# A second level of Strassen's form in the output product of a fused attention and SwiGLU kernel

## The chip, the core and the metric

The kernel runs on one core of one Trainium2 chip. A core has engines that run side by side: TensorE (PE in the profile, with its weight loads as PEld), VectorE (DVE), ScalarE (ACT), GpSimd (POOL), and SyncE (SP), whose queue issues nearly all DMA transfers here. Each engine takes its instructions in the order of the program and waits on semaphores for the others. The metric is the device time of one execution in microseconds (us); lower is better.

## The reference, cut to what matters

```python
# q, k, v: (8, 12, 448, 64) float32; g_q, g_k: (64,)
def rmsnorm(x, g):
    return x / np.sqrt(np.mean(x * x, axis=-1, keepdims=True) + 1e-06) * g
q_n, k_n = rmsnorm(q, g_q), rmsnorm(k, g_k)
scores = (1.0 / np.sqrt(64)) * np.matmul(q_n, k_n.transpose(0, 1, 3, 2))
attn = softmax(scores)
x = np.matmul(attn, v).transpose(0, 2, 1, 3).reshape(3584, 768)
# w_gate, w_val: (768, 1536); w_out: (1536, 768)
xn = x / np.sqrt(np.mean(x * x, axis=-1, keepdims=True) + 1e-06) * rms_g
g = xn @ w_gate
val = xn @ w_val
out = (g * (1.0 / (1.0 + np.exp(-g))) * val) @ w_out
```

All of it is float32. The weights arrive as float64 and are made float32 on the chip.

## The kernel before

The work is one attention block over 8 sequences (b = 0 to 7) of 448 tokens with 12 heads, taken as 48 pairs of heads (g), and one feed-forward block over the same tokens. The order of TensorE's work is written by hand: `pe(fn)` (L382) runs one step and counts it, `after(n, fn)` (L379) places a piece of work of another engine n steps later, and `fill` (L1155) puts feed-forward steps between the attention steps of a pair, as many as their cost asks for. While sequence b is in attention, the output product of sequence b-2 and then the gate and value products of sequence b-1 are worked off. In the last 200 us there is no attention left: the output product of sequence 6, the gate and value products of sequence 7 and its output product follow one another.

Gate and value products (`quad`, L907) use Strassen's form with one level: seven products p1 to p7 instead of eight, each of 12 matmuls 128 x 128 by 224 columns. One step is one product. The seven right-hand blocks per hidden chunk, with the sums T1 to T4 made once in sequence 1 (`derive`, L845), lie in DRAM in `kept` and are streamed for each sequence.

The output product (`out_strassen`, L1041) does the same with pairs of 128-token tiles: seven products, each of six matmuls by 384 columns, for two pairs in most sequences. `out_pairs` (L805) names the tiles; sequences 0 and 4 finish one pair only and carry the rest on, so sequences 2, 3, 5, 6 and 7 have four tiles each, and so has sequence 1. The left sums S1 to S4 are made on VectorE while the gate products run (`sums`, L975 to L986, for each of the six hidden chunks). Results leave PSUM through VectorE or ScalarE (L1059, L1066, L1064, L1073) and go to DRAM by L1028.

The hidden values h lie in 14 tiles that are taken from a list and given back (`free_h`, L705). Weights pass through 25 blocks of 128 x 384 (`free_w`, L706), two more once the conversion has ended. `uses` (L814) is the fixed list of all blocks that will be wanted; `ask` (L824) sends the next loads as long as more than four blocks stay free, and `used` (L890) gives a block back one step after its last matmul. PSUM has three banks for the feed-forward products (`ps_f`, L369). GpSimd adds the exponentials for the softmax sums (L555, L562), makes the powers of the norms (L506) and scales q (L511).

Of the kernel before, what the change touches and what calls it, by code (L numbers as in the profile page):

```python
# [8 lines left out]
F32 = mybir.dt.float32  # L9
# [16 lines left out]
BW = 384  # L26
# [309 lines left out]
def safe_scores(  # L336
# [25 lines left out]
    NW, NH = 25, 14  # L362
    const, small = pool("c_const", 1), pool("c_small", 4)
    qk_pool, v_pool, qn_pool, qkT_pool = pool("c_qk", 4), pool("c_v", 3), pool("c_qn", 1), pool("c_qkT", 2)
    e_pool, tmp, y_pool, rest_pool = pool("c_e", 11), pool("c_tmp", 1), pool("c_y", 2), pool("c_rest", 2)
    x_pool, s_pool, slots = pool("c_x", 4), pool("c_xs", 3), pool("c_slots", 1)
    raw_pool, cv_pool = pool("c_raw", 7), pool("c_cv", 4)
# [330 lines left out]

    def block_of(n, fc):

        return f"B{fc // NFP + 1}{n + 1}", fc % NFP
# [3 lines left out]
    free_h = [slots.tile([128, 512], F32, name=f"h{i}") for i in range(NH)]  # L705
    free_w = [slots.tile([128, BW], F32, name=f"w{i}") for i in range(NW)]  # L706

    def block():

        if free_w:  # L710
            return free_w.pop(0), free_w
        return free_h.pop(0), free_h

    def room(n):
        return len(free_w) + max(len(free_h) - 4, 0) >= n
# [48 lines left out]
    room_so, carried = [], []  # L764
    TURNS = len(pieces) + 7

    def home(key):
        if key[0] == "w":
            return kept[key[2], NAMES.index(key[3]), key[4]]
        return kept_o[NAMES.index(key[2]), key[3]]  # L770
# [4 lines left out]
    def convert():  # L775

        n = turn_of["n"]
        if n >= TURNS or not room(1):
            return False
        turn_of["n"] += 1  # L780
        if 0 <= n - 5 < len(pieces):
            key = pieces[n - 5][0]
            st[key] = block()
            lo, top = st.pop(("cv", n - 5))
            nc.gpsimd.tensor_tensor(data(key).bitcast(I32), top, lo, ALU.add)
        if 0 <= n - 4 < len(pieces):
            st["cv", n - 4] = join(*st.pop(("cv", n - 4)))
        if 0 <= n - 3 < len(pieces):
            st["cv", n - 3] = split(st.pop(("raw", n - 3)), n - 3)
        if n < len(pieces):  # L790
            st["raw", n] = load_raw(pieces[n][1])
        if 0 <= n - 7 < len(pieces):
            keep(pieces[n - 7][0])
        if turn_of["n"] == TURNS:

            free_w.extend(cv_pool.tile([128, BW], F32, name="top") for _ in range(2))
            whole = [raw_pool.tile([128, 2 * BW], F32, name="raw") for _ in range(7)]
            room_so.extend(whole[:6])
            homes = [whole[6][:, 0:BW], whole[6][:, BW:]] + [cv_pool.tile([128, BW], F32, name="top") for _ in range(2)]
            carried.extend(t[:, i * 128:(i + 1) * 128] for t in homes for i in range(3))  # L800
        return True
# [12 lines left out]
    uses = []  # L814
    for b in range(1, B):
        for fp in range(NFP):
            uses += [("w", b, fp, name, w) for name in (("B12", "B11", "B22", "B21") if b == 1 else ORDER) for w in range(2)]
            if b == 1:
                uses += [("wd", b, name, fp) for name in BLOCKS]
        uses += [("wo", b, name, c) for name in ORDER_O for c in range(NFP)]  # L820
# [3 lines left out]
    def ask():  # L824

        if turn_of["n"] < TURNS:
            return
        while asked["n"] < len(uses):
            key = uses[asked["n"]]
            keep_free = 4  # L830
            if key[1] == 1 and key[0] in ("w", "wd"):
                fp = key[2] if key[0] == "w" else key[3]
                keep_free = max(7 + 8 * fp - asked["derived"], 1)
            elif asked["derived"] < len(derived):
                return
            if key[0] == "wo" and key[2][0] == "T" and asked.get("sums_o", 0) < 4 * NFP:
                return
            if len(free_w) <= keep_free:
                return
            asked["n"] += 1  # L840
            asked[key] = now["t"]
            st[key] = block()
            nc.sync.dma_start(out=data(key), in_=home(key))
# [45 lines left out]

    def used(key):  # L890
        give_back(key)
        after(1, ask)
# [14 lines left out]
    def quad(b, fp):  # L907
# [21 lines left out]
        def rows(fc):  # L929
            return st["h", b, fc][:, shift:shift + S]  # L930

        def p1():
            bank["a"] = product(b, fp, "A11", "B11")
# [7 lines left out]
        def p2():  # L941
            product(b, fp, "A12", "B21", onto=bank["a"])
            for fc in (fp, fp + NFP):
                st["h", b, fc] = free_h.pop(0)
                if ("h", b - 1, fc) in st:

                    before = st.pop(("h", b - 1, fc))
                    if b % 2:
                        nc.gpsimd.tensor_copy(st["h", b, fc][:, 0:64], before[:, S - 64:S])
                    if carries(b - 1):  # L950
                        at = out_pairs(b - 1)[-1][1] + 1
                        nc.gpsimd.tensor_copy(carried[fc], before[:, at * 128:(at + 1) * 128])
                    free_h.append(before)
# [21 lines left out]
        def sums(pair):  # L975

            st["left_sums"] = now["t"]
            if pair < len(out_pairs(b)):
                if fp == 0:
                    st["so", b, pair] = {name: room_so[3 * pair + i].rearrange("p (c n) -> p c n", c=NFP)  # L980
                                         for i, name in enumerate(("S1", "S2", "S4"))}
                of = lambda name: left_o(b, pair, name, fp)
                nc.vector.tensor_tensor(of("S1"), of("A21"), of("A22"), ALU.add)
                nc.vector.tensor_tensor(of("S2"), of("S1"), of("A11"), ALU.subtract)
                nc.vector.tensor_tensor(of("S3"), of("A11"), of("A21"), ALU.subtract)
                nc.vector.tensor_tensor(of("S4"), of("A12"), of("S2"), ALU.subtract)  # L986

        def p3_last():
            p3()
            after(3, lambda: sums(0))  # L990
            after(5, lambda: sums(1))
# [5 lines left out]
    def project_out(b, n, i, part, last):  # L997
# [5 lines left out]
        for fc in range(part * each, (part + 1) * each):  # L1003
            nc.tensor.matmul(ps, lhsT=st["h", b, fc][:, i * 128:(i + 1) * 128], rhs=data(("wo", b, *block_of(n, fc))),  # L1004
# [25 lines left out]

    def left_o(b, pair, name, c):

        if name in ("S1", "S2", "S4"):
            return st["so", b, pair][name][:, c, :]
        row, col = (2, 1) if name == "S3" else (int(name[1]), int(name[2]))
        i, fc = out_pairs(b)[pair][row - 1], c + (col - 1) * NFP
        return carried[fc] if i < 0 else st["h", b, fc][:, i * 128:(i + 1) * 128]
# [3 lines left out]
    def out_strassen(b):  # L1041
# [45 lines left out]
        def step(name, which, half, last):  # L1087
# [5 lines left out]
            for c in range(3 * half, 3 * half + 3):  # L1093
# [5 lines left out]
                if last and b % 4 == 3 and name in ("T3", "T4"):  # L1099
                    free_h.append(st.pop(("h", b, c + (name == "T4") * NFP)))  # L1100
# [9 lines left out]

    def plain(fc):
# [3 lines left out]
        h = lambda: st["h", 0, fc][:, 0:S]  # L1115

        def step(w, half):
# [10 lines left out]
            if w == 0:  # L1128
                st["h", 0, fc] = free_h.pop(0)
# [14 lines left out]
    def out_items(b):  # L1144
        if b >= FIRST_O:
# [9 lines left out]
    def fill(n=None):  # L1155
# [8 lines left out]
        for _ in range(min(n, len(todo))):  # L1164
# [13 lines left out]
            if now["t"] - st["block"] > 4 and now["t"] != st.get("left_sums"):  # L1178
                left = 3 - sum(derive() for _ in range(3))
                for _ in range(left):  # L1180
                    derive_o()

# [219 lines left out]
```

## Time and profile before

| what | value |
|---|---|
| runs | 1598.54, 1598.49 and 1596.86 us, median 1598.49 |
| span of the profiled execution, first to last instruction | 1595.3 us, so that some 3.2 us of the median lie around it |
| granted TensorE clock | 0.999 |
| VectorE, ScalarE, GpSimd busy | 55%, 29%, 41% of the span |
| DMA | 273.28 MB, mean 171 GB/s |
| weight blocks loaded for gate and value, 192 KB each | 511 and 41 from `kept` |
| weight blocks loaded for the output product, 192 KB each | 296 and 22 from `kept_o` |
| median time from issue to landing of such a load | 2.6 to 2.9 us |
| median time of a store of such a block | 3.8 us to `kept`, 3.5 us to `kept_o` |

How to read the profile: the first figure of a group is its busy time in us, the second the mean duration of one instruction in ns. A float32 matmul of the program is two TensorE instructions with a weight load each. Durations of TensorE instructions overlap, so the time from one to the next is taken from runs of many. In a timeline a row gives the start, the length of the merged run, the engine, the line and what ended the idle time ahead of it.

### The profile page before, as it was taken

The page shows a single profiled execution, that of the slowest core. Times are in us where ns is not written, and L with a number is a line of the kernel's source. Part 1 is how long each engine was busy: PE and PEld are TensorE (multiplying, and loading weights), DVE is VectorE, ACT ScalarE, POOL GpSimd, SP SyncE. Part 2 cuts the span into 40 slices and gives each one's busy share as a digit, 9 for nine tenths or more (in the row PEclk, how much of TensorE's full clock was granted, in tenths as well). Part 3 has the DMA queues.
Part 4 walks back from the last instruction along what each step waited for, and adds up shares of the span by engine and source line. Part 5 has one row for each costly group of instructions (what it writes and reads, how often), then busy time and mean ns, then how long its engine had stood idle before and what let it go on. Part 6 is the DMA issues. An engine that isn't in the chain of part 4 may idle for free.

```text
span 1595.3 us, 21559 instructions
## 1 busy us (share of the span) xinstructions
PE 1571.9 (99%) x7286; PEld 1113.4 (70%) x7286; DVE 872.6 (55%) x1556; ACT 470.3 (29%) x940; POOL 660.1 (41%) x712
## 2 busy tenths in 40 slices
PE   8999999999999999999999999999999999999998
PEld 4344445687756887578865788667885688759974
DVE  6889898578822556236562354635563355613531
ACT  6746563232222222222232222323322222101010
POOL 6867877465334443344333443344542342000000
PEclk9999999999999999999999999999999999999999
DMA  7648474957746554465544655584554544456651
GB/s 207 209 148 260 162 252 125 287 188 242 250 142 204 154 156 121 140 205 156 154 119 143 204 154 148 149 267 131 161 145 124 176 141 139 119 178 212 174 151 55
DMA packets 261996, 273.28 MB, mean 171 GB/s; under 512 B 78836, under 2 KB 258804, under 8 KB 261876
## 3 DMA queue, kind: packets, MB, share of 16 engines
q1 hardware_dynamic: 260948, 271.61, 56.6%
q8 instruction: 60, 0.98, 0.3%
q14 instruction: 60, 0.49, 0.1%
q10 hardware_dynamic: 800, 0.20, 0.1%
q0 software_dynamic: 128, 0.00, 0.0%
HBM read 232.40 MB, written 39.32 MB: 170 GB/s over the span
## 4 chain that ended last, share of the span: by engine, by line
PE 78%; DVE 7%; DMA 1%; issue 1%; POOL 0%; SPq 0%; ACT 0%; DVEq 0%; POOLq 0%
PE ff L902 39%; PE ff L1094 22%; PE sc L545 6%; PE av L597 5%; PE sc L575 2%; PE den L610 2%; PE tr L527 1%; DVE top L747 1%; DVE top L748 1%; DVE top L746 1%; PE ff L1004 1%; DVE rd L618 1%; DVE h L925 0%; DVE h L924 0%; DMA w<-kept_o 0%
## 5 line engine op out<-in xcount | busy, mean ns | idle before, releaser
L902 PE MATMUL ff<-x,w 128*128 128x224 f32 x1878 | 381.5, 354 | 0.1
L902 PEld LDWEIGHTS ff<-x,w 128*128 128x128 f32 x1878 | 351.3, 190 | 15.3 <-issue 11.7
L555 POOL TENSOR_TENSOR es<-e 128x448 f32<-128x448 f32 x82 | 91.7, 1141 | 492.0 <-ACT e L549 492.0
L902 PE MATMUL ff<-xs,w 128*128 128x224 f32 x1374 | 281.7, 353 | 4.4 <-DVE w L858 2.9
L902 PEld LDWEIGHTS ff<-xs,w 128*128 128x128 f32 x1374 | 258.0, 190 | 8.7 <-issue 6.0
L562 POOL TENSOR_TENSOR es<-es,e 64x448 f32<-64x448 f32 (+1 forms) x164 | 191.9, 1181 | 6.3
L618 DVE RECIPROCAL rd<-rd 128x448 f32<-128x448 f32 x41 | 121.0, 2952 | 113.7 <-ACT rd L617 113.7
L549 ACT ACTIVATE e<-sc,rs 128x448 f32<-128x448 f32 x288 | 161.6, 635 | 50.2 <-PE sc L545 47.8
L1094 PE MATMUL ff<-w,h 128*128 128x384 f32 x498 | 167.8, 487 | 0.6 <-ACT p L1073 0.6
L1094 PE MATMUL ff<-w,raw 128*128 128x384 f32 x468 | 159.5, 487 | 0.3 <-DVE y L1066 0.3
L545 PE MATMUL sc<-qT,kT 64*128 64x448 f32 x576 | 138.0, 572 | 1.9 <-ACT e L549 0.7
L1094 PEld LDWEIGHTS ff<-w,h 128*128 128x128 f32 x498 | 93.5, 190 | 64.5 <-issue 1.3
L1094 PEld LDWEIGHTS ff<-w,raw 128*128 128x128 f32 x468 | 87.6, 190 | 60.9 <-issue 2.6
L597 PE MATMUL av<-e,vt 128*64 128x448 f32 x576 | 118.8, 548 | 0.0
L506 POOL TENSOR_TENSOR rs<-ms,mhalf 128x12 f32<-128x12 f32 (+1 forms) x50 | 114.6, 2292 | 4.2
L1122 PE MATMUL ff<-x,w 128*128 128x448 f32 x288 | 111.8, 541 | 0.0
L545 PEld LDWEIGHTS sc<-qT,kT 64*128 64x128 f32 x576 | 53.9, 185 | 82.5 <-issue 68.5
L914 DVE TENSOR_TENSOR cc<-ff,u 128x448 f32<-128x448 f32 x84 | 52.3, 623 | 87.3 <-PE ff L902 87.2
L597 PEld LDWEIGHTS av<-e,vt 128*64 128x64 f32 x576 | 37.1, 136 | 75.6 <-issue 74.2
L1122 PEld LDWEIGHTS ff<-x,w 128*128 128x128 f32 x288 | 53.3, 190 | 50.8 <-issue 49.0
L631 POOL TENSOR_TENSOR ss<-ss,rd 128x448 f32<-128x448 f32 x40 | 46.6, 1165 | 82.7 <-ACT rd L630 82.7
L935 ACT COPY p<-ff 128x448 f32<-128x448 f32 x42 | 22.4, 533 | 192.6 <-PE ff L902 192.6
(132 smaller groups left out, 1860.9 us busy)
## 6 DMA issues: line engine op xcount, KB each, us to landing
w<-kept SPq DMA_DIRECT2D x511, 192.0 KB, 2.6
w<-kept_o SPq DMA_DIRECT2D x296, 192.0 KB, 2.9
kept<-w SPq DMA_DIRECT2D x89, 192.0 KB, 3.8
qk<-in_q_dram SPq DMA_DIRECT2D x48, 192.0 KB, 3.0
qk<-in_k_dram SPq DMA_DIRECT2D x96, 96.0 KB, 3.3
vt<-in_v_dram SPq DMA_DIRECT2D x48, 192.0 KB, 2.5
raw<-in_moe_w_gate_dram SPq DMA_DIRECT2D x24, 384.0 KB, 4.5
raw<-in_moe_w_val_dram SPq DMA_DIRECT2D x24, 384.0 KB, 4.5
```

The source lines that it names most:

```text
L506: nc.gpsimd.tensor_tensor(st["rs", g][:, cols], ms, mhalf[:, cols], ALU.pow)
L545: nc.tensor.matmul(ps[:, 0:S], lhsT=kT[r, c * 128:(c + 1) * 128], rhs=qT[r, :], start=True, stop=True)
L549: nc.scalar.activation(e, ps[:, 0:S], ACT.Exp, scale=rs[:, n:n + 1])
L555: nc.gpsimd.tensor_tensor(es, st["e", g, 0, j], st["e", g, 1, j], ALU.add)
L562: nc.gpsimd.tensor_tensor(es[r], es[r], e[r], ALU.add)
L597: nc.tensor.matmul(av[own(j), 0:S], lhsT=vt[:, j, c], rhs=st["e", g, c, j], start=False, stop=(c == NK - 1), skip_group_check=True)
L618: nc.vector.reciprocal(rd, rd)
L631: after(1 if soon else 4, lambda: (nc.gpsimd.tensor_tensor(ss, ss, rd, ALU.add), st.update({("summed", b): hp})))
L902: nc.tensor.matmul(bank[:, w * HT:(w + 1) * HT], lhsT=wt[:, c * 128:(c + 1) * 128], rhs=x[:, c, :], start=onto is None and w == c == 0, st ...
L914: nc.vector.tensor_tensor(add[name], ps[:, 0:S], add[other], ALU.add)
L1094: nc.tensor.matmul(ps, lhsT=left_o(b, which, LEFT_O[name], c), rhs=data(("wo", b, name, c)), start=first and c == 0, stop=c == NFP - 1, sk ...
L1122: nc.tensor.matmul(bank[w][:, 0:S], lhsT=data(key)[:, c * 128:(c + 1) * 128], rhs=st["x", 0, half][:, c, :], start=half == c == 0, stop=ha ...
```

## The change

Sequences 2, 3, 5, 6 and 7 get a new output product, `out_quads`. The four tiles are the rows of one matrix product 512 x 1536 by 1536 x 768. It is cut by Strassen's form into seven products of 256 x 768 by 768 x 384, and each of these again into seven of 128 x 384 by 384 x 192. That makes 49 products of three matmuls with 192 columns. Sequences 1 and 4 keep the old form.

The steps of the seven outer products i are interleaved: a(0), b(0), c(0), a(1), d(0), b(1), c(1), a(2), d(1) and so on. Each of a, b and c makes two inner products into the two halves of one PSUM bank; d adds the last inner product to the second half of the bank of c. VectorE draws the inner results together, GpSimd adds the outer ones, and the left sums of the inner level (`left_q1`) are made by VectorE between these steps, one outer product ahead.

The right-hand pieces of both levels are made once, in the gate stage of sequence 2 (`derive_q`): 21 jobs load two blocks each from `kept_o`, make four subtractions of 192 columns, and store seven half blocks to `kept_q`. The loads of `kept_q` wait until all 21 jobs are stored.

Besides, h gets fixed places (`hs`, four tiles of three chunks), so that the copies for the next sequence are made for three chunks at a time at the start of the gate stage; the left sums of the outer level are made for three chunks at a time, after the third and the sixth chunk; there are 23 weight blocks instead of 25, three q and k buffers instead of four, three output buffers instead of two, and five new ones for the inner left sums.

```diff
-    NW, NH = 25, 14
+    NW = 23
-    qk_pool, v_pool, qn_pool, qkT_pool = pool("c_qk", 4), pool("c_v", 3), pool("c_qn", 1), pool("c_qkT", 2)
-    e_pool, tmp, y_pool, rest_pool = pool("c_e", 11), pool("c_tmp", 1), pool("c_y", 2), pool("c_rest", 2)
+    qk_pool, v_pool, qn_pool, qkT_pool = pool("c_qk", 3), pool("c_v", 3), pool("c_qn", 1), pool("c_qkT", 2)
+    e_pool, tmp, y_pool, rest_pool = pool("c_e", 11), pool("c_tmp", 1), pool("c_y", 3), pool("c_rest", 2)
...
+    HW, KG = BW // 2, 3
+    ORDER_Q = ("B11", "B21", "T2", "T3", "T4", "T1", "B22")
...
-    free_h = [slots.tile([128, 512], F32, name=f"h{i}") for i in range(NH)]
+    hs = [slots.tile([128, KG, 512], F32, name=f"h{g}") for g in range(NFC // KG)]
...
     for b in range(1, B):
         for fp in range(NFP):
+            for at, name in enumerate(("B12", "B11", "B22", "B21") if b == 1 else ORDER):
+                uses += [("w", b, fp, name, w) for w in range(2)]
+                if b == 2 and at % 2 == fp % 2:
+                    n = sum(key[0] == "wx" for key in uses) // 2
+                    if n < len(jobs_q):
+                        i, j = jobs_q[n]
+                        uses += [("wx", b, ORDER_Q[i], c) for c in (j, j + KG)]
...
+            if key[0] == "wq" and asked.get("sums_q", 0) < len(jobs_q):
+                return
...
+    def derive_q(wait=3):
...
+        nc.vector.tensor_tensor(tb[:, 1], x[:, 1], x[:, 0], ALU.subtract)
+        nc.vector.tensor_tensor(ta[:, 1], y[:, 1], x[:, 1], ALU.subtract)
+        nc.vector.tensor_tensor(ta[:, 0], y[:, 1], tb[:, 1], ALU.subtract)
+        nc.vector.tensor_tensor(tb[:, 0], y[:, 0], ta[:, 0], ALU.subtract)
+
+        def store():
+            parts = kept_q[i].rearrange("p (n w) -> p n w", w=HW)
+            nc.sync.dma_start(out=parts[:, j], in_=x[:, 0])
+            for src, first, second in ((y, 1, 6), (ta, 2, 3), (tb, 4, 5)):
+                gap = (second - first) * KG
+                nc.sync.dma_start(out=parts[:, first * KG + j:second * KG + j + 1:gap], in_=src)
...
+        after(1, store)
+        for key in (*keys, own_a, own_b):
+            after(3, lambda key=key: used(key))
...
         def p1():
+            if fp < 2:
+                for g in (fp, fp + 2):
+                    if carries(b - 1):
+                        nc.gpsimd.tensor_copy(carried[g], group(out_pairs(b - 1)[-1][1] + 1, g))
+                    if b % 2:
+                        nc.gpsimd.tensor_copy(hs[g][:, :, 0:64], hs[g][:, :, S - 64:S])
...
         def p3_last():
+            if fp == NFP - 1 and in_quads(b):
+                after(1, lambda: left_q1(b, 0, range(3)))
             p3()
-            after(3, lambda: sums(0))
-            after(5, lambda: sums(1))
+            if fp % KG == KG - 1:
+                after(3, lambda: sums(0))
+                after(4 if fp == NFP - 1 else 5, lambda: sums(1))
...
+        def add(to, one, other):
+            for row in range(2):
+                nc.gpsimd.tensor_tensor(to[row], one[row], other[row], ALU.add)
+
+        def finish(i):
+            name, m = ORDER_Q[i], dst[i]
+            if name == "B21":
+                add(m, m, dst[0])
+                out(m, 0, 0)
...
+            elif name == "T1":
+                add(dst[3], dst[3], m)
+                add(m, m, dst[2])
+                out(dst[3], 1, 2)
+            elif name == "B22":
+                add(m, m, dst[5])
+                out(m, 1, 0)
...
+        def two(i, what):
+            ps = bank[i, what] = ps_f.tile([128, 512], F32, name="ff", tag="f")[:, 0:BW].rearrange("p (h n) -> p h n", h=2)
+            for h in range(2):
+                term(i, 2 * "abc".index(what) + h, ps[:, h], start=h == 0)
+            return ps
...
+        def a(i):
+            ps = two(i, "a")
+            dst[i] = rows(ORDER_Q[i])
+            q1 = st["q1", b, i] = tmp.tile([128, S], F32, name="th", tag="th", bufs=2)[:, 0:HW]
+            nc.scalar.copy(q1, ps[:, 0])
+            nc.vector.tensor_tensor(lo_hi(dst[i][0])[0], ps[:, 1], q1, ALU.add)
+
+        def bb(i):
+            ps = two(i, "b")
+            u = st["u", b, i] = tmp.tile([128, S], F32, name="th", tag="th", bufs=2)[:, 0:BW].rearrange("p (h n) -> p h n", h=2)
+            nc.vector.tensor_tensor(u[:, 0], ps[:, 0], st.pop(("q1", b, i)), ALU.add)
+            nc.vector.tensor_tensor(u[:, 1], ps[:, 1], u[:, 0], ALU.add)
+            left_q1(b, i, (3,))
+
+        def c(i):
+            ps = two(i, "c")
+            u3 = st["u", b, i][:, 1:2].to_broadcast([128, 2, HW])
+            nc.vector.tensor_tensor(dst[i][1].rearrange("p (h n) -> p h n", h=2), ps, u3, ALU.add)
+            if i + 1 < len(ORDER_Q):
+                left_q1(b, i + 1, range(3))
+
+        def d(i):
+            ps = bank[i, "c"]
+            term(i, 6, ps[:, 1], start=False)
+            nc.vector.tensor_tensor(lo_hi(dst[i][0])[1], ps[:, 1], st.pop(("u", b, i))[:, 0], ALU.add)
+            finish(i)
+
+        full = 2 * KG * HW
+        if b == B - 1:
+            steps.append((0, idle))
+        for i in range(len(ORDER_Q) + 1):
+            if i < len(ORDER_Q):
+                steps.append((full, lambda i=i: a(i)))
+            if i:
+                steps.append((full // 2, lambda i=i - 1: d(i)))
+            if i < len(ORDER_Q):
+                steps += [(full, lambda i=i: bb(i)), (full, lambda i=i: c(i))]
+        return steps
```

## The prediction

> **What bounds the kernel now.** I read the busy shares first, then the chain that ended last, then the stages, then single stretches of the timeline.
>
> ```profile
> span 1595.3 us, 21559 instructions
> ...
> PE 1571.9 (99%) x7286; PEld 1113.4 (70%) x7286; DVE 872.6 (55%) x1556; ACT 470.3 (29%) x940; POOL 660.1 (41%) x712
> ...
> PE 78%; DVE 7%; DMA 1%; issue 1%; POOL 0%; SPq 0%; ACT 0%; DVEq 0%; POOLq 0%
> ```
>
> TensorE is the bound: 99% busy, with 23 us idle in all. Fewer TensorE columns are time won, as long as nothing else comes late. The chain in order of time shows two stages without attention, the gate products of sequence 7 and its output product, as unbroken runs:
>
> ```profile
> 1438.65 95.34 PE ff L902 x504
> 1533.99 54.20 PE ff L1094 x168
> ```
>
> One instruction of 224 columns follows another after 95.34/504 = 189.2 ns, one of 384 columns after 54.20/168 = 322.6 ns. That is 0.834 ns a column and 2.4 ns fixed, so 192 columns should take 162.5 ns, if the weight load allows it. A load lasts 190 ns in the rows of both lines, but loads overlap: in the warm-up, matmuls of 128 columns,
>
> ```profile
> 7.34 1.20 PEld L1241 LDWEIGHTS warm<-ident 128*128 128x128 f32 x10
> ```
>
> ten loads take 1.20 us, one every (1.20 - 0.19)/9 = 112 ns. So 162.5 ns stands.
>
> The stages tell how full the other engines are. Columns: stretch, its length, busy time of PE, PEld, DVE, ACT, POOL (instructions), clock, DMA share, GB/s.
>
> ```profile
> 493.50:625.60 132.10, 131.59 (x702) 110.59 (x701) 70.44 (x132) 36.47 (x73) 55.69 (x61) 1.00 0.54 159
> 625.60:691.00 65.40, 65.40 (x242) 35.26 (x241) 25.12 (x42) 15.37 (x29) 21.83 (x23) 1.00 0.50 146
> 1534.00:1588.20 54.20, 54.17 (x168) 31.56 (x167) 9.45 (x22) 2.49 (x5) 0.00 (x0) 1.00 0.30 88
> ```
>
> The first is the gate stage of sequence 2, the second its output stage with attention between, the third the output stage of sequence 7 alone. VectorE has room in output stages, the DMA engines nowhere are full. The fullest stretch of DMA is
>
> ```profile
> 285.00:290.00 5.00, 5.00 (x29) 1.70 (x29) 2.49 (x5) 1.70 (x3) 0.00 (x0) 1.00 1.01 362
> ```
>
> so about 362 GB/s is the most seen; at the mix of the gate stage, 159 GB/s at a share of 0.54, full would be 294 GB/s. Last, what VectorE does where an output stage begins (sequence 3):
>
> ```profile
> 822.96 0.62 DVE L914 TENSOR_TENSOR cc<-ff,u 128x448 f32<-128x448 f32 x1 [1.65 <-PE ff L902]
> ...
> 824.22 2.45 DVE L663 SCALAR_TENSOR_TENSOR x<-x,rg,rb 128x448 f32<-128x448 f32 x4
> ...
> 832.69 0.85 DVE L680 TENSOR_TENSOR x<-x 128x672 f32<-128x672 f32 x1
> 833.46 0.85 DVE L680 TENSOR_TENSOR xs<-x,xs 128x672 f32<-128x672 f32 x1
> 836.75 2.95 DVE L618 RECIPROCAL rd<-rd 128x448 f32<-128x448 f32 x1 [2.45 <-ACT rd L617]
> ```
>
> From 822.96 to 834.3 it is busy without a gap with the norm of the next sequence; today no output product needs it early.
>
> [...]
>
> **The change part by part.** TensorE: an output stage of four tiles has 84 matmuls, 168 instructions, 54.2 us. The new one has 147, so 294 x 162.5 ns = 47.8 us. Five sequences: 5 x 6.4 = **32.0 us** off the bound.
>
> Start of each new output stage. VectorE works in order, and before the drain of c(0), which lets d(0) add to its bank, and of d(0), whose bank a(2) takes, the changed order of instructions puts the norm of the next sequence (six of L663, four of L680), the second half of the outer left sums (eight additions of 384) and the inner ones. From one start to the next, by the timeline above and its neighbours: 0.60 us for L663, 0.77 for L680, 0.47 for a 384-wide addition, 0.60 if it needs the one before, 0.27 for a 192-wide drain, 2.87 for the reciprocal. Counted from the last gate product: c(0) is drained at 11.7 us, a(1) at 16.3, and behind the L680s, the reciprocal of the attention group and L625 comes d(0), drained at 22.6. TensorE: 0.4 transposes, then a, b, c, a to 8.2, attention 6.7 (830.99 to 837.72 in the timeline) to 14.9, d(0), b(1), c(1) to 19.8; a(2) then waits 2.9 us. After that VectorE needs 4.2 us of work for every 6.8 us of TensorE and catches up. So 2.9 us in sequences 2, 3 and 5. In 6 there is no attention to cover: d(0) waits from 8.2 to 11.9, c(1) 1.5 and d(1) 0.6 more, **5.8 us**. In 7 there is no norm either: 0.5 + 0.9 = 1.4. Together 3 x 2.9 + 5.8 + 1.4 = **15.9 us**. Bounds: 8 if VectorE's gaps close better, 25 if they take the longer times that a like row shows (L858 678 ns in the mean against 550).
>
> Rest of these stages: b(i+1) has 0.6 us to spare for its inner left sums, and kT copies and reduces of attention stand among them: 0 to 6 us over five stages, I take 2.5.
>
> GpSimd: 14 additions of some 1.09 us per stage, 15 us. The last two come, in 2, 3 and 5, behind the softmax sums and powers of the last attention group (six at 1.15, 2.3, two at 0.5), and the gate product p1 that follows copies into a tile they still read; p2 waits for that copy. Summed along its queue this is 1.4 us late: **4.2 us** in all (0 to 8). In 6 and 7 GpSimd is idle otherwise.
>
> End: today the last matmul is followed by one drain of 0.56 us, then the stores. Now a drain and two GpSimd additions: 0.36 + 2.2 + 0.3 for the handing over, **+2.3 us**.
>
> Gate stage of sequence 2: 42 loads of 192 KB and 84 stores of 21 x 672 KB, 22.7 MB on top of 159 GB/s x 132.1 us = 21.0 MB, less some 4 MB of output blocks no longer asked ahead: 39.5 MB, 299 GB/s in 132 us. That is full by the one measure, 83% by the other. The order of loads against matmuls shows it too: before, a gate block is asked for 28 to 37 us of TensorE time ahead in this stage, now mostly 9 to 15, because the jobs hold four blocks each, and just before three attention groups only 7.2, 1.9 and 0.4 us ahead. A load lands after 2.6 us at best and queues behind stores that wait for VectorE. I take 2 + 3 us for these two and 2 for crowded transfers (together 0 to 18). Its 84 subtractions of about 0.36 us are 30 us on VectorE (70.4 busy of 132.1, less 8 that the joined left sums save), in bursts of eight to twelve; such bursts in sequence 1 cost TensorE 2.9 us ("PE ff L902 <- DVE w L858"): 3 again.
>
> Output stage of sequence 2: no block can be asked for before the jobs are stored; the first is asked for 0.4 us before its use. 3 us late, half of which VectorE uses to catch up: 1.5 (1 to 6). In the other stages the blocks are 10 us ahead or more, and 14.5 MB in 48 to 60 us stay under the 362; nothing.
>
> Two weight blocks fewer in sequence 1, already short there: 1 (0 to 4). The three q and k buffers cost nothing: the buffer that pair g+3 takes was last read by the transposes of pair g, a stage earlier. Third output buffer, fixed h, joined copies: nothing while TensorE is the bound.
>
> Sum: 15.9 + 2.5 + 4.2 + 2.3 + 7 + 3 + 1.5 + 1 = 37.4 us against 32.0: span 1600.7, and with the 3.2 us around it **1604 us**, 0.3% more.
>
> **Rivals.** A, faster: the wait at the starts does not form. VectorE's queue ahead of d(0) is 22.6 us and needs to be 19.8 or less; for it speaks that many of these operations are independent and overlap, and that a late load lets VectorE run ahead; against it, that L680 and the reciprocal are measured at their shortest here. With 5 us at the starts, 3 in the gate stage of 2 and 10 elsewhere: 1598.5 - 32.0 + 18 = 1584.5. It decides from 32 us of losses down. B, much slower: DMA becomes the bound of sequence 2. Its gate and output stages move some 39.5 + 19 MB; at 294 GB/s that is 199 us, against 132 + 59 for TensorE; with loads behind stores and every attention group short of blocks, 20 us more than forecast, 1622. For it the share of 0.54 at 159 GB/s, against it 362. C: the weight load holds 192 columns at its 190 ns: 294 x 190 = 55.9 us, no gain at all, 1598.5 + 8.4 + 37 = 1644. The 112 ns of the warm-up speak against it.
>
> **How the numbers follow.** Forecast 0.50 (own range 1597 to 1612), A 0.27, B 0.18, C 0.05. A difference under 0.2%, 3.2 us, can't be told from none. Faster: A but for its edge, 0.25; same: the low edge of the forecast and the high one of A, 0.15; slower 0.60. The range from 1584 to 1624 leaves out the lower half of A, the upper part of B, and C.
>
> **What would show it.** Right: output products of 192 columns at 162 to 163 ns in unbroken runs; waits of TensorE for VectorE's drains (c(0) or d(0)) at the starts of the five output stages, longest in sequence 6; a DMA share over 0.9 in the gate stage of 2 with TensorE waiting for blocks; ScalarE's p1 copy waiting for GpSimd. Wrong: spacing near 190 ns, starts without waits, or waits for blocks in the later stages, where I see none.

## The result: 0.5% slower, and the profile after

The changed kernel took 1605.76 us (median of six runs, 1601.32 to 1610.14) against 1597.74 us for the kernel before (six runs, 1596.64 to 1599.6): 1.0049 times as long, 95% interval 1.0031 to 1.0067. The forecast was 1604 us. The executions of the changed kernel lie 9 us apart, those of the kernel before 3 us.

The profiled execution took 1601.32 us. From the busy shares and the chain of waits of its page:

```profile
span 1599.5 us, 23661 instructions
...
PE 1550.0 (97%) x7916; PEld 1197.5 (75%) x7916; DVE 983.5 (61%) x1697; ACT 472.9 (30%) x955; POOL 724.0 (45%) x718
...
PE 74%; DVE 10%; DMA 1%; issue 1%; POOL 0%; ACT 0%; DVEq 0%; SPq 0%; POOLq 0%; ACTq 0%
```

TensorE has 22 us less to do, but 26 us more in which it is idle (1599.5 - 1550.0, before 1595.3 - 1571.9), and VectorE has gone from 7% to 10% of the chain. The chain in order of time still shows unbroken runs of TensorE:

```profile
1225.11 8.78 PE ff L1269 x54
...
1444.70 95.35 PE ff L982 x504
1551.95 36.36 PE ff L1269 x222
```

8.78/54 is 162.6 ns for one instruction of 192 columns: the 162.5 ns of the prediction, and no hold by the weight load. (36.36/222 is 163.8 ns, because the first two starts lie 0.27 us apart and the full 0.33 us of the last instruction are in it.) So the whole gain is there; that the busy time falls by 22 us and not by 32 is in part the half clock shown below, since slowed work counts as busy (1.00 of each slice at a clock of 0.50 there). Where the gain goes is seen from the lengths of the stages, from the first gate (or output) product of each to that of the next stage, read off the timelines of TensorE:

| stage | before, us | changed, us | gain expected | given back |
|---|---|---|---|---|
| gate products of sequence 2 | 128.2 | 131.6 | 0 | 3.3 |
| output product of sequence 2 | 69.6 | 67.7 | 6.4 | 4.5 |
| output product of sequence 3 | 69.6 | 72.2 | 6.4 | 9.0 |
| output product of sequence 5 | 69.6 | 72.8 | 6.4 | 9.7 |
| output product of sequence 6 | 54.2 | 54.4 | 6.4 | 6.6 |
| output product of sequence 7 | 54.3 | 50.4 | 6.4 | 2.4 |
| last matmul to the end | 7.1 | 9.3 | 0 | 2.1 |

The other stages are 1.5 us shorter in sum, so that the losses of this execution, the fastest of the six, come to 36.1 us. The 3.3 us of the first row end with 1.55 us in which TensorE waits for the first block of the output product. The output stages lose what they gained. The start of one shows how: the timeline of sequence 3, TensorE, VectorE and GpSimd (start, duration, engine, line; in brackets the idle time and what ended it):

```profile
837.83 2.84 POOL L555 TENSOR_TENSOR es<-e 128x448 f32<-128x448 f32 x2 [16.45 <-ACT e L549]
837.86 1.82 DVE L680 TENSOR_TENSOR xs<-x 128x672 f32<-128x672 f32 x1
...
839.82 2.11 PE L1269 MATMUL ff<-w,h 128*128 128x192 f32 x12
839.87 1.52 DVE L680 TENSOR_TENSOR xs<-xs,x 128x672 f32<-128x672 f32 x1
840.63 3.45 POOL L562 TENSOR_TENSOR es<-es,e 128x448 f32<-128x448 f32 x2
841.30 1.78 DVE L680 TENSOR_TENSOR x<-x 128x672 f32<-128x672 f32 x1
841.77 1.14 PE L1269 MATMUL ff<-w,l 128*128 128x192 f32 x6
843.01 1.78 DVE L680 TENSOR_TENSOR xs<-x,xs 128x672 f32<-128x672 f32 x1
844.71 2.94 DVE L618 RECIPROCAL rd<-rd 128x448 f32<-128x448 f32 x1
847.76 0.62 DVE L625 TENSOR_TENSOR x<-av,rd 128x448 f32<-128x448 f32 x1
848.30 0.34 DVE L1308 TENSOR_TENSOR p<-ff,th 128x192 f32<-128x192 f32 x1
...
848.70 3.59 PE L1269 MATMUL ff<-w,raw 128*128 128x192 f32 x12 [5.79 <-DVE p L1308]
```

Three things are to be seen. a(2) waits 5.79 us for the drain of d(0) (L1308), which stands behind the norm's additions and the reciprocal, as forecast. The additions L680 take 1.5 to 1.8 us, twice the 0.85 of before, and beside them GpSimd adds the softmax sums. And after the wait twelve matmuls take 3.59 us, where the twelve at 839.82 take 2.11. The busy times by stretches show why (busy PE, PEld, DVE, ACT, POOL, then the clock granted to TensorE):

```profile
848.00:849.00 1.00, 0.30 (x1) 0.30 (x2) 0.90 (x3) 0.58 (x1) 0.00 (x0) 0.55 0.00 0
849.00:850.00 1.00, 1.00 (x4) 1.00 (x4) 0.96 (x4) 0.00 (x0) 0.00 (x0) 0.50 0.00 0
850.00:851.00 1.00, 1.00 (x5) 1.00 (x4) 0.97 (x3) 0.00 (x0) 0.00 (x0) 0.50 0.00 0
851.00:852.00 1.00, 1.00 (x6) 1.00 (x6) 0.95 (x2) 0.00 (x0) 0.00 (x0) 0.74 0.57 157
852.00:853.00 1.00, 1.00 (x8) 1.00 (x7) 0.28 (x1) 0.63 (x2) 0.00 (x0) 1.00 0.11 40
```

The clock is 0.50 for some 3.4 us, and the 192-column instructions in it start 0.32 us apart in place of 0.163. Such stretches stand behind three waits (sequences 3, 5 and 6; the one in 5 is twice as long). Summed over slices of 1 us, TensorE worked 9.8 us of them at half clock, so its work took 4.9 us longer.

### The profile page after: what moved, and what is told of

It is laid out like the page before. It is cut to its first block, busy times and chain, and to the rows that moved or that the text cites. A ratio compares the mean times of both kernels' runs of the same rounds, so it can differ in the third digit from the quotient of the medians.

```text
span 1599.5 us, 23661 instructions
## 1 busy us (share of the span) xinstructions
PE 1550.0 (97%) x7916; PEld 1197.5 (75%) x7916; DVE 983.5 (61%) x1697; ACT 472.9 (30%) x955; POOL 724.0 (45%) x718
## 3 DMA queue, kind: packets, MB, share of 16 engines
q8 instruction: 65, 1.06, 0.3%
## 4 chain that ended last, share of the span: by engine, by line
PE 74%; DVE 10%; DMA 1%; issue 1%; POOL 0%; ACT 0%; DVEq 0%; SPq 0%; POOLq 0%; ACTq 0%
PE ff L982 41%; PE ff L1269 11%; PE sc L545 5%; PE ff L1201 5%; PE av L597 5%; PE sc L575 2%; PE ff L1077 2%; PE den L610 2%; PE tr L527 1%; DVE rd L618 1%; DVE xs L680 1%; DVE l L1144 1%; DVE top L762 1%; DVE x L663 1%; DVE top L763 1%
## 5 line engine op out<-in xcount | busy, mean ns | idle before, releaser
L982 PEld LDWEIGHTS ff<-x,w 128*128 128x128 f32 x1854 | 346.2, 190 | 17.1 <-issue 9.1
L982 PE MATMUL ff<-xs,w 128*128 128x224 f32 x1416 | 288.7, 353 | 3.2 <-DVE w L904 2.9
L982 PEld LDWEIGHTS ff<-xs,w 128*128 128x128 f32 x1416 | 266.4, 190 | 5.6 <-issue 4.7
L562 POOL TENSOR_TENSOR es<-es,e 64x448 f32<-64x448 f32 (+1 forms) x164 | 196.4, 1208 | 6.3
L1269 PE MATMUL ff<-w,l 128*128 128x192 f32 x580 | 109.5, 332 | 7.5 <-DVE c L1301 3.6
L1269 PEld LDWEIGHTS ff<-w,l 128*128 128x128 f32 x580 | 97.2, 193 | 12.1 <-DVE y L1301 4.3
L1334 PEld LDWEIGHTS ff<-x,w 128*128 128x128 f32 x288 | 53.3, 190 | 50.8 <-issue 49.0
L1241 POOL TENSOR_TENSOR y<-y,p 128x384 f32<-128x384 f32 x10 | 10.0, 998 | 165.1 <-DVE y L1308 157.2
L1001 ACT ACTIVATE th<-c 128x224 f32<-128x224 f32 x42 | 16.3, 389 | 230.9 <-DVE c L994 230.8
L1269 PE MATMUL ff<-w,raw 128*128 128x192 f32 x356 | 68.3, 341 | 12.9 <-DVE p L1308 12.5
```

Source lines behind the costliest of these rows:

```text
L562: nc.gpsimd.tensor_tensor(es[r], es[r], e[r], ALU.add)
L982: nc.tensor.matmul(bank[:, w * HT:(w + 1) * HT], lhsT=wt[:, c * 128:(c + 1) * 128], rhs=x[:, c, :], start=onto is None and w == c == 0, st ...
L1269: nc.tensor.matmul(ps, lhsT=a[:, j, :], rhs=data(key)[:, n % 2 * HW:(n % 2 + 1) * HW], start=start and j == 0, stop=j == KG - 1, skip_grou ...
L1334: nc.tensor.matmul(bank[w][:, 0:S], lhsT=data(key)[:, c * 128:(c + 1) * 128], rhs=st["x", 0, half][:, c, :], start=half == c == 0, stop=ha ...
```

## The experiments

Each is the changed kernel but for the edit shown; e5 to e12 have the edit of e1 as well, and e8, e10 and e11 also those of e7. Of longer edits only the decisive lines are shown. Times are medians in us, ratios are to the kernel before on the same chip. The kernels of e3, e5 and e6 leave out work that the result needs; they show what that work costs.

| run | us (range) | ratio, 95% interval |
|---|---|---|
| e0_same | 1605.26 (1601.35 to 1606.49) | 1.0044 [1.0030, 1.0058] |
| e1_norm_sums_late | 1586.14 (1585.68 to 1587.98) | 0.9932 [0.9915, 0.9948] |
| e2_softmax_adds_late | 1597.84 (1596.40 to 1603.72) | 1.0004 [0.9995, 1.0013] |
| e3_no_inner_weight_sums | 1606.55 (1606.00 to 1608.04) | 1.0059 [1.0043, 1.0076] |
| e4_busy_waits | 1601.01 (1599.59 to 1604.95) | 1.0024 [1.0016, 1.0032] |
| e5_late_no_inner_sums | 1579.48 (1578.84 to 1579.64) | 0.9885 [0.9869, 0.9902] |
| e6_late_no_subtractions | 1580.93 (1580.34 to 1581.46) | 0.9896 [0.9880, 0.9913] |
| e7_late_and_end | 1586.66 (1584.13 to 1589.27) | 0.9937 [0.9920, 0.9953] |
| e8_s4_early | 1584.37 (1583.27 to 1584.56) | 0.9917 [0.9900, 0.9934] |
| e10_half_on_gpsimd | 1593.64 (1591.99 to 1597.86) | 0.9979 [0.9972, 0.9986] |
| e11_stores_on_act | 1603.05 (1602.60 to 1603.88) | 1.0038 [1.0023, 1.0052] |
| e12_best | 1579.02 (1578.82 to 1579.18) | 0.9884 [0.9868, 0.9901] |

### VectorE's order at the starts (e1)

```diff
-            after(NPAIR // 2 + i, lambda args=args: op(*args))
+            after((NPAIR // 2 + i) if not in_quads(b - 1) else 12 + 2 * i, lambda args=args: op(*args))
```

> The four 672-wide additions of the next sequence's norm stand behind the drains of d(0) and d(1) instead of ahead of d(0). Theory Q (VectorE's queue at the starts, and the half clock that follows a wait): d(0) is drained 6.6 us earlier in sequences 3 and 5 and 3.3 us earlier in 6, so the waits 5.8, 5.8, 3.4 and 0.9 us go, and with them some 6 to 9 us of TensorE at half clock: 1583 to 1588 us. Rival S (VectorE's time is short over the whole output stage, not at the start): the same waits come back one or two drains later, 1600 us or more. Rival L (the blocks of sequence 2 set the loss): within 3 us of the changed kernel.

Four additions per stage moved, no work removed: 19 us faster than the changed kernel (e0), 12 faster than the kernel before. VectorE's timeline of sequence 3 has d(0)'s drain 6.6 us earlier in the stage (841.66 - 823.06 against 848.30 - 823.13), ahead of the additions:

```profile
838.07 2.94 DVE L618 RECIPROCAL rd<-rd 128x448 f32<-128x448 f32 x1
841.66 0.35 DVE L1308 TENSOR_TENSOR p<-ff,th 128x192 f32<-128x192 f32 x1
845.50 0.85 DVE L680 TENSOR_TENSOR xs<-x 128x672 f32<-128x672 f32 x1
```

The output stages of 3 and 5 fall from 72.2 and 72.8 to 65.0 us and keep only a wait of 0.70 at their ends. The wait of 3.37 in sequence 6 stayed, with its half clock: it is for c(0)'s drain, which stands behind other work (the scalings L663). Rivals S and L fall. e12, which moves the scalings in sequence 6, no longer has the wait of 3.37.

### GpSimd beside VectorE (e2)

```diff
-            n = 3 if g == NPAIR + 1 else 2
+            start = g % NPAIR == 1 and g > 2 * NPAIR and in_quads(g // NPAIR - 2)
+            n = 3 if g == NPAIR + 1 else 6 if start else 2
```

What is tested is whether the additions L680 are long because GpSimd's additions run beside them.

> Only GpSimd's softmax additions of the attention group at each start stand later, behind the two additions that finish d(1); VectorE's order is untouched. Theory P: the four 672-wide additions took 1.5 to 1.8 us each in sequences 3 and 5 instead of 0.85 [...]. Then they take 0.85 again, d(0) is drained 3.6 us earlier, the two waits of 5.8 shrink to about 2.2 (the 2.9 of the forecast), with less time at half clock: 8 to 12 us faster than the changed kernel, 1594 to 1598. Rival: the additions are slow for a reason of their own (their operands, the semaphores), then they stay at 1.5 to 1.8 and the time is the same within 2 us, or worse if the softmax sums come too late for their attention group.

VectorE's order is that of the changed kernel, and still the additions (here L681) are short again and the wait shrinks:

```profile
840.41 0.85 DVE L681 TENSOR_TENSOR xs<-x 128x672 f32<-128x672 f32 x1
...
842.98 0.85 DVE L681 TENSOR_TENSOR xs<-x,xs 128x672 f32<-128x672 f32 x1
```

```profile
847.74 2.22 PE L1270 MATMUL ff<-w,raw 128*128 128x192 f32 x12 [2.29 <-DVE p L1309]
```

2.29 us is nearly the 2.9 of the forecast, and no half clock follows it in this profile (0.998 in the mean; others of the twelve executions go down to 0.993). 7.4 us are won, though a new wait of 1.47 us for an inner left sum (VectorE's, once per stage) appears in 2, 3 and 5. So the neighbour on GpSimd doubled the additions: 0.85 us became 1.5 to 1.8. The trace of the changed kernel shows it over all its sequences: the 14 of L680 with nothing on GpSimd beside them take 0.85 to 0.86 us, the eight that lie wholly beside its 448-wide additions 1.47 to 1.82. Two with only its int32 additions (L803) beside them take 0.85 too, and the 384-wide additions L1301, which read a PSUM bank, take 0.55 to 0.56 us with GpSimd's 448-wide additions beside them or without. What it is in the neighbour that counts is not shown.

### What a wait costs beyond itself (e0, e4)

> The changed kernel once more, nothing altered, to see how far its executions lie apart and why. In its profile each long wait at a start (5.8 us in sequences 3 and 5) is followed by 3 to 6 us in which the clock granted to TensorE is 0.50 and twelve 192-column instructions take 3.59 us instead of 2.11. If the spread of 1601 to 1610 us comes from there, an execution near 1608 shows the same waits and more time at 0.50 behind them (about 7 us more lost to it), and the clock's mean is lower by 0.003. If it comes from transfers, the waits for blocks in sequence 2 are longer by that much and the clock is the same.

The profiled execution of e0 (span 1603.5 us, 4.0 more than the first) has the same waits of 5.79 us, but 6.8 us of half clock behind each of those two and 3.4 behind the one in sequence 6: 7.2 us lost against 4.9. The output stage of sequence 2, with a wait of 2.68 for d(0) where there was one of 0.92, is 1.0 us longer, and the end of the kernel 1.1. For e4 TensorE was kept busy in the waits:

```diff
         def a(i):
+            if i == 2 and b in (3, 5):
+                busy(20)
             ps = two(i, "a")
...
         def d(i):
+            if i == 0 and b == 6:
+                busy(12)
             ps = bank[i, "c"]
```

> The changed kernel with its waits left as they are, but TensorE multiplies the identity in them (20 extra products of 128 columns, some 4.5 us, ahead of a(2) in sequences 3 and 5, 12 ahead of d(0) in 6; nothing reads them). Theory H: a wait costs twice, once for itself and once because the clock granted to TensorE falls to half for 3.4 or 6.8 us after it. Then d(0) is drained as late as before, a(2) starts at the same moment, but at full clock: no half clock behind the starts, the 4.9 to 7.2 us lost to it come back, 1598 to 1601 us, and the executions lie within 3 us of each other instead of 9. Rival: the half clock has another cause (a fixed period, the load of the chip): it stays and the time stays at 1605, or grows by what the extra products take.

```profile
844.07 4.63 PE L1287 MATMUL busy<-ident 128*128 128x128 f32 x40
850.03 2.22 PE L1269 MATMUL ff<-w,raw 128*128 128x192 f32 x12 [1.34 <-DVE p L1317]
```

a(2) starts 25.6 us after the stage's first product, exactly as before (850.03 - 824.45; 848.70 - 823.13), but its twelve matmuls take 2.22 us instead of 3.59. From 12 us on the profile has no half clock left before the last matmul, and 3 to 4 us (by the differences to the kernel before on the same chip) are won by useless work. In sequence 6 nothing is won: without the half clock TensorE reaches the next drain early and waits 1.28 us for it, and the stage takes 54.4 us as before. The range did not shrink to the 3 us expected: it is still 5 (15 runs). The executions over 1602 us have mean clocks of 0.995 to 0.996, those under 1601 us 0.997 to 0.998, so a half clock remains in some; where, no trace shows.

The stretches of half clock at the starts last 3.41 or 6.83 us. In all fourteen traces the clock changes, up to the last matmul, lie on a grid of 3.413 us that starts with the first record of full clock. Of the windows of this grid at full clock, each of the 17 in which TensorE was busy, by the trace, for 1.41 us or less was followed by half clock, none with 1.68 us or more was, and between the two both occur. At half clock, the ten windows with 2.66 us of work or less were followed by another at half clock, those with 2.83 us or more by full clock. So it matters where a wait falls: in e2 and e6 the wait of 3.37 us in sequence 6 lies across two windows (1.60 and 1.86 us busy in e2), and no half clock follows; in e1 a wait as long lies mostly in one (0.66 us busy), and it does.

### The gate stage of sequence 2 (e3, e5, e6)

```diff
-                if b == 2 and at % 2 == fp % 2:
+                if False:
...
-            return kept_q[key[2]][:, 2 * HW * key[3]:2 * HW * key[3] + n]
+            return kept_o[key[2], key[3] % NFP][:, 0:n]
```

> Leaves out the inner sums of the output weights in sequence 2 (their 42 loads, 84 subtractions and 84 stores); the output products read the undivided blocks in their place, the same number of loads of the same size. The prediction priced this work at 11.5 us (7 for blocks, 3 for VectorE, 1.5 at the output stage): then 1594. The stage lengths of the profile say 3.3 us in the gate stage and 2.6 to 3.6 us in the output stage of sequence 2: then 1598 to 1600, 6 to 7 us below the changed kernel. If the transfers were the bound of sequence 2 (rival B), 15 us or more: 1590 or below. The waits at the starts of sequences 3, 5, 6 and 7 stay as they are.

No gain at all. The gate stage became 4.3 us shorter (127.25 us), but the output stage 5.9 us longer: its first blocks are now in time, so TensorE reaches a(2) early and waits the full 5.79 us there, with 6.8 us of half clock after it. Late blocks and the late drain had stood in for each other. With the drain in time (the edit of e1 added), the price can be read:

> The kernel with the norm's additions late, and without the inner sums of the output weights in sequence 2 (left out, as in e3_no_inner_weight_sums). There, late blocks in sequence 2 and the wait at its start stood in for one another: without the sums the gate stage of 2 was 4.3 us shorter and its output stage 5.9 us longer. With the wait at the start gone, the whole price of the inner sums must show: 4.3 us in the gate stage and 1.7 us for the first blocks of the output stage, 1579 to 1581 against 1586.1. If they cost nothing in truth: 1586.

6.7 us by the medians, and 5.3 by the stages (gate stage 131.9 to 127.25, output stage 65.7 to 65.0); 1.8 us of difference lie ahead of sequence 1's gate stage, where the two kernels do the same. They come from the start: in e1 the clock is at 0.50 from 8.0 to 11.5 us, in e5 it is not. Next, the subtractions by themselves:

> The kernel with the norm's additions late, leaving out only the 84 subtractions on VectorE of the inner sums; their loads and stores stay. The prediction split the gate stage of 2 into 7 us for blocks and transfers and 3 for VectorE's bursts. If VectorE's share holds at 3 of 10, this is 1 to 1.5 us faster than 1586.1, and the wait for a gate block (1.9 us) and the one for the first output block (1.7 us) stay. If the subtractions delay the stores and so the blocks, both waits shrink too: 1581 to 1583. If transfers alone matter: 1586.

5.2 us, with the same two stages as e5 (127.25 and 65.0). So the subtractions make the whole loss. Busy times by stretches of e1, then of e6:

```profile
560.00:600.00 40.00, 38.07 (x204) 33.00 (x203) 28.75 (x63) 9.99 (x20) 14.06 (x13) 1.00 0.90 288
600.00:629.00 29.00, 28.25 (x157) 23.30 (x157) 17.23 (x37) 8.89 (x18) 13.05 (x12) 1.00 0.93 300
```

```profile
560.00:600.00 40.00, 40.00 (x216) 35.28 (x215) 20.51 (x36) 9.97 (x20) 13.35 (x13) 1.00 0.95 300
600.00:625.00 25.00, 25.00 (x141) 20.27 (x140) 11.19 (x18) 8.12 (x16) 12.33 (x12) 1.00 1.02 330
```

In e6 the DMA engines are fuller (share 0.95 to 1.02) and TensorE waits for nothing. What holds it in e1 is seen in SP's queue just before the late gate block (599.86 us, 1.93 us of wait); the same block in e6 below it:

```profile
583.81 6.29 SPq L962 DMA_DIRECT2D kept_q<-w  x2
590.20 0.46 SPq L962 DMA_DIRECT2D kept_q<-top  x1
...
595.48 1.52 SPq L962 DMA_DIRECT2D kept_q<-w  x3
597.09 1.44 SPq L889 DMA_DIRECT2D w<-kept  x3
```

```profile
587.19 1.53 SPq L957 DMA_DIRECT2D kept_q<-w  x3
590.14 1.94 SPq L889 DMA_DIRECT2D w<-kept  x3
```

The gate loads (L889) stand behind stores that wait for VectorE's subtractions, 6.29 us for two of them, and are issued 7 us later. The two stores end at 590.10; the last of the four subtractions ahead of them (L955) runs from 589.73 to 590.09.

### Attempts on what was left (e7, e8, e10, e11, e12)

e7 and e12 move the scalings of the norm in sequence 6 as well; e7 also changes the end of each stage:

```diff
-                after(hp // 2, lambda hp=hp: scale(hp))
+                after(hp // 2 if b < B - 1 else 6 + 2 * hp, lambda hp=hp: scale(hp))
...
+            if i == len(ORDER_Q) - 1:
+                steps.append((full // 2, lambda i=i: d(i)))
+            steps.append((full, lambda i=i: c(i)))
```

> The kernel with the norm's additions late, and three more edits: in sequence 6, which has no attention to cover its start, the six scalings of the norm stand behind the first drains too; the last product of each stage adds its d into a bank of its own ahead of c, so that the last three matmuls no longer wait for c's drain (0.71 us in each of five stages); and at the very end one of the two additions stands on VectorE. Theory Q: 3.4 us of wait and 1.7 of half clock in sequence 6, 3.5 us at the ends of the stages, 1 us at the end of the kernel: 1575 to 1578 us. Rival S (VectorE's time is short further on): the scalings come back as waits later in sequence 6, 1581 or more.

The output stage of sequence 6 fell from 54.1 to 50.6 us, but the last product now waits 1.5 to 2.0 us in each stage where it waited 0.71: no gain in sum, against the 1575 to 1578 us expected. The trace names no cause for this wait; the one I took, S4, was tested:

```diff
-                left_q1(b, i + 1, range(3))
+                left_q1(b, i + 1, range(4 if i + 2 == len(ORDER_Q) else 3))
```

> As e7_late_and_end, where the last d stood ahead of c but then waited 1.5 to 2.0 us for the inner left sum S4 that VectorE had only just made. Here S4 of the last product is made with the other three, one product earlier. If that was the wait: 1.5 to 2.0 us in each of five stages go, 1577 to 1579 us. If VectorE is then late with the drains of the last product instead, the wait stays under another name and the time stays at 1586.

In sequences 6 and 7 the wait went; in 2, 3 and 5 it came back as 1.48 us for another drain (that of a), and behind it the wait of ScalarE's p1 copy for GpSimd, which the prediction had named, cost TensorE 0.84 us each. So 1584.4 us, not the 1577 to 1579 expected. Two attempts on the stores of sequence 2, on top of e8:

> As e8_s4_early, with every second set of four subtractions of the inner weight sums on GpSimd in place of VectorE. Theory V (VectorE's bursts hold the stores, and the loads of gate blocks stand behind these stores in SP's queue): half as long a burst, the loads are issued earlier, 2 to 3 us faster than e8_s4_early. Rival: GpSimd takes longer for each (its 384-wide addition takes 1.0 us, VectorE's 0.55) [...], so the stores come as late or later: no gain, or up to 4 us slower.

> As e8_s4_early, with the 84 stores of the inner weight sums issued from ScalarE's queue in place of SP's; VectorE's subtractions stay where they are. If the loads of gate blocks come late because they stand in SP's queue behind stores that wait for VectorE, the waits for blocks in sequence 2 (1.7 us for a gate block, 1.4 and 0.6 for the first output blocks) go without any work being taken away: 4 to 6 us faster than e8_s4_early, unless ScalarE, waiting for VectorE with a store at its head, hands over its tanh results late. If it is VectorE's time as such that is missing: no gain.

Both lost. In e10 the gate stage took 144.5 us where e8 has 132.1, with waits of 3.68 and 4.19 us for gate blocks and 6 us lost to half clock; SP's stores wait there up to 7.0 us for GpSimd and up to 8.6 us for VectorE. In e11 no block is late, which speaks once more for SP's queue as the cause, but ScalarE, with stores at the head of its queue, is late (TensorE waits 12.1 us for it, 4.95 of them for one of its copies, and 6 us more are lost to half clock; gate stage 151.4 us). e12 keeps what paid, with one row's last addition made while d runs:

> The kernel with the norm's additions late, and of the later edits only the two that paid: in sequence 6 the norm's scalings stand behind the first drains too (there e7_late_and_end's output stage was 3.5 us shorter than with the additions late alone), and at the very end one row's addition is made on GpSimd while d runs and the other on VectorE (1 us). The order a, d, b, c, d of the last product stays, with its 0.71 us of wait, in place of the 1.5 to 2.0 us that the other order cost. Theory Q: 1580.5 to 1582.5 us, 0.985 to 0.987 of the kernel before's reference fast runs, i.e. 1.0% below it. If the executions of sequence 6 come out as with e7 but the end hides nothing: 1583.

```diff
+                    nc.vector.tensor_tensor(m[0], m[0], dst[5][0], ALU.add)
...
+            if b == B - 1 and i + 1 == len(ORDER_Q):
+                nc.gpsimd.tensor_tensor(dst[i][1], dst[i][1], dst[5][1], ALU.add)
```

1.2% faster than the kernel before. Against e1 the output stage of 6 is 4.3 us shorter. The end is 0.8 shorter, but with unchanged code it lasts 9.3 us in one execution and 10.3 in another, so this isn't shown to be a gain. Another 1.7 us lie ahead of sequence 1's gate stage (295.2 us against 296.9), where the kernels are alike, so that these are no gain of the edits and account for 1579 us where 1580.5 to 1582.5 was expected.

What differs there is the clock at the start. In the six profiles with 296.8 to 297.0 us (e1, e2, e4, e6, e8, e10) part of the warm-up's products in the first 12 us go at half pace: ten of them take 2.15 us in e1 and 1.28 in e12, and TensorE is 1.6 us behind by 16 us. In e2, e6 and e10 full clock is first on record at 10.4 to 10.7 us, elsewhere at 4.2 to 6.2 us. In e1, e4 and e8 it is given up again after one window of the grid: a wait of 1.9 to 2.0 us for a load leaves 1.41 to 1.53 us of work in that window, where the runs without the delay have 1.58 or more. The times of the kernel before fall into two groups 1.6 us apart as well (on e1's chip 1596.64 to 1597.05 and 1598.16 to 1598.78, none between); that this is the same cause is likely, not shown.

## Why the prediction came out right, and which steps did not

The time and the sign held, in good part by luck: errors of both signs nearly cancel. Losses of 37.4 us were forecast. The profiled execution has 36.1, but it is the fastest of the six; by the medians (8.0 us slower) it is 40.0. The 3.2 us around the span were too many as well: they set the span of one execution against the median of others, and wherever a run of the kernel before lists both, 1.7 to 1.9 us lie between. With these the same sum gives 1602.5 us in place of 1604. Step by step, from the profiled execution:

- **Gain of 32.0 us, at 162.5 ns: right.** Rival C is out.
- **Starts, 15.9 us: right in sum and in the mechanism, wrong in the parts.** VectorE's waits are 16.6 us (0.92, 5.79, 5.79, 3.36, and 0.73 in sequence 7; predicted 2.9, 2.9, 2.9, 5.8, 1.4). The step that failed is the 0.77 us taken for each L680 "at their shortest": beside GpSimd's additions four of them take 6.85 us from the first start to the reciprocal instead of 3.1. e2 shows it. In sequence 2 late blocks gave VectorE the time (e3). In sequence 6 the second wait of 1.5 us did not come, because the half clock held TensorE back; where the clock stays full, in e2 and e4, it is there with 1.3 us.
- **Not in the sum at all: the half clock after a wait,** 4.9 to 7.2 us of slower work. e4 shows it. The time grows by less, because in sequence 6 the slower work fills a later wait.
- **Rest of these stages, 2.5 us:** no wait for left sums in b was found; instead the last d waits 0.71 us for c's drain in all five stages, 3.5 us, and some 6 us more lie in short pauses: in sequence 7 single instructions start 0.20 to 0.27 us apart in place of 0.163, several of them just after a wait. This term was far too small.
- **GpSimd at the stage ends, 4.2 us: nothing here,** since the stages end later than GpSimd. e8, where they end earlier, has it, at 0.84 us each. An addition takes 1.00 us, not 1.09, which is near the mean of the int32 additions of before (L785, 1087 ns).
- **End, +2.3: 2.1,** in e0's execution 3.2.
- **Gate stage of 2, 7 + 3 us: 1.8,** the 3.3 of the table without the wait for the first output block, and with the cause turned round. The crowded transfers cost nothing (e6); VectorE's bursts cost all of it, through stores that hold SP's queue.
- **First blocks of the output stage of 2, 1.5 us: 2.6** (1.55 and 1.06). Sequence 1, +1: it is 1 us shorter.

Of the signs named, the spacing and the waits for drains came, and a DMA share of 0.93 in the gate stage of 2 with waits for blocks. That the waits would be longest in sequence 6 did not come (3.36 us against 5.79 in 3 and 5), nor did ScalarE's copy waiting for GpSimd.

Of the rivals, A named the point from which it decides, losses of 32 us: they were 36 to 40. Nor was VectorE short of time: a place in its queue was worth 19 us. B falls with e6.

Left open: the spread of the executions. In the six runs of the changed kernel the longest has a mean clock of 0.990 and the shortest 0.993, by estimate some 10 us more at half clock, or 5 of the 8.8 us between them. That the grid of windows lies differently against the program each time would do this; without traces of the other executions it is not shown, and the rest has no cause here. Moving the subtractions of sequence 2 to stages with room on VectorE was not tried.

## What to carry to other kernels

When a tuned kernel gets shorter on its bounding engine, look at who works in order ahead of the first results it needs: moving four additions that nobody awaits was worth more than half of the saved matmul time. Where VectorE's order moves, price its additions of two SBUF tensors by their time beside GpSimd (here 1.5 to 1.8 us), not by their shortest (0.85). And take care with experiments that remove one of two waits in a row: the second may fill the gap, as in e3.

## What was not expected of the hardware

The clock granted to TensorE was halved, mostly for 3.41 or 6.83 us and in e11 once for 10.2, and after waits of 1.9 to 2.0 us too: what counted in these traces was the work in a window of a fixed grid of 3.41 us, 1.41 us or less for half clock to follow, 2.83 us or more for it to end. Behind a wait of 5.8 us this added 1.4 to 3.0 us of slowed work. Filling 4.63 us of the wait with products that nobody reads took the extra away. A 672-wide addition of two SBUF tensors on VectorE took 0.85 us alone and 1.5 to 1.8 us beside GpSimd's 448-wide additions, which themselves took 1.4 to 1.7 us instead of 1.14.
